# A decode attention kernel with its maximum one chunk later, one wait a head on VectorE, and K0 in one load

## The chip, the cores and the metric

The kernel runs on one core of a Trainium2 chip. The metric is the device time of one execution in microseconds. The kernel before takes 318.31 us, the median of three runs (318.19 to 318.35). The core has a matrix engine (TensorE, PE in the profile), a vector engine (VectorE, DVE), a scalar engine (ScalarE, ACT), GpSimd (POOL), and a queue engine (SyncE, SP) that here issues all loads of K and V. Each works through its own instructions in order; they meet through semaphores.

## What is computed

One query row per head attends to 8192 keys, for 16 heads of width 256, in bfloat16:

```python
B, H, Sq, Sk, D = 1, 16, 1, 8192, 256
def reference(q, k, v):
    scale = q.shape[-1] ** -0.5
    scores = jnp.einsum("bhqd,bhkd->bhqk", q, k) * scale
    p = _softmax(scores, axis=-1)
    return jnp.einsum("bhqk,bhkd->bhqd", p, v)
```

K and V of one head are 4 MB each and are used once, so 134 MB are read.

## The kernel before

A head's keys lie on 128 partitions, 64 keys on each. K and V have two buffers each, by the parity of the head. The SyncE queue issues the loads in the order of the list `ORDER` (L16); it waits, ahead of K(h), until VectorE (semaphore `kd`) and GpSimd (`tp`) have finished head h−2, and ahead of V(h) until TensorE's sum of iteration h is done (`pr`). A wait there holds all loads behind it. `CUTS` (L15) splits some loads into pieces: K0 and K15 after 34 of 64 keys, V13, V14 and V15 in other places. The second piece of a K has the semaphore `kb`.

**The scores.** Of the 64 keys of a partition, the first 24 go to GpSimd and ScalarE: GpSimd multiplies four keys at a time by the head's q row into one of two `prod` buffers (L186, six groups a head), and ScalarE sums each key's products into the score tile S (L398, four instructions a group, then semaphore `sp`). The other 40 go to VectorE: four chunks (index c) of ten fused multiply-and-sum instructions (L212), each chunk followed by semaphore `kd`.

**The maximum.** When VectorE has ended its four chunks, it waits for its own last chunk and for ScalarE's last group and takes the maximum of each partition (L229, semaphore `m`). TensorE turns it into a row (L332, `mT`); VectorE reduces that to one number g (L203, function `xmax`) behind the first chunk of the next head; TensorE spreads it over the partitions (L317, `bc`); ScalarE takes the exponent (L363, function `expo`) in the next head's loop of groups, behind group i = 1.

**The output.** TensorE's iteration h spreads the maximum of head h−1 (L317), multiplies the exponents of head h−2 with V (L270, 32 matmuls), sums the exponents of head h−1 (L257, "the sum"), runs a filler (L281), then waits for ScalarE's `collect` (L374), which copies the product out of PSUM, and gathers its rows (L294). Only then does it wait for the maximum of head h, turn it (L331, L332), and make the broadcast q row of head h+2 (L247). ScalarE's iteration h begins with `q_copy`, the copy of the q row of head h+1 (L392 and L354), which TensorE makes at the end of its iteration h−1; then come the six groups, with `expo` and `final` (L380, the scaled output of an earlier head) between them, and `collect` at the end. The last head's V comes in four pieces, and its last 36 keys are added directly to the output rows (L339).

**The waits at a head's start.** The function `k_waits` (L142 to L144) waits for the q row (`qb`) and for the two K semaphores. VectorE runs it in every chunk (L208), with a further wait for `kb` (L209), and GpSimd in every pair of groups (L183). For head 15, the wait on `kb` passes in the first chunk (c = 0) with K0's second piece alone, and asks for K15's second piece from c = 1 on.

Of the kernel before, what the change touches and what calls it, by code (L numbers as in the profile page):

```python
# [5 lines left out]
ALU = mybir.AluOpType  # L6
ACT = mybir.ActivationFunctionType
AX = mybir.AxisListType
# [13 lines left out]
AHEAD = {"k1": 16, "kb": 16, "sp": 2, "pr": 1, "cm": 2, "pv": 1, "fin": 3, "rc": 3, "ex": 1, "mT": 1, "g": 1, "nb": 1}  # L22
STREAM_AHEAD = ("v0", "v1", "v0_40", "v1_48")


def bass_standalone__mha_softmax__decode_kernel(nc: bass.Bass, q: bass.AP, k: bass.AP, v: bass.AP, out: bass.AP):
# [28 lines left out]
    with contextlib.ExitStack() as ctx:  # L55

        def sb(name, shape, d):
            return ctx.enter_context(nc.sbuf_tensor(name, shape, d))
# [31 lines left out]
        lsum = sb("lsum", [P, 1], FP32)  # L90
        recip = sb("recip", [WIDE, H], FP32)
# [3 lines left out]
        ones_col = sb("ones_col", [P, 1], FP32)  # L95
        o_all = sb("o_all", [WIDE, LAST * HW], out.dtype)
        o_last = sb("o_last", [1, D], out.dtype)

# [5 lines left out]
        qrow = ps("qrow", [P, 2 * 512])  # L104
        spare = ps("spare", [P, 512])

        for name in ("pool", "cb", "cf", "ldq", "qp", "qb", "tp", "sp", "kd", "m", "mT", "g", "bc", "nb", "ex"):
            sem(name)
        for name in ("rc", "pr", "cm", "pv", "fin", "o"):
            sem(name)  # L110
# [30 lines left out]
        def k_waits(e, h):  # L141
            e.wait_ge(sem("qb"), h + 1)  # L142
            e.wait_ge(sem("k0"), h // 2 * 16 + 16)  # L143
            e.wait_ge(sem("k1"), (h + 1) // 2 * 16 + 16)  # L144

        @(lambda f: f(nc.gpsimd))
        def _(pool):
            def step(ins, n):
                ins.then_inc(sem("pool"), 1)
                pool.wait_ge(sem("pool"), n)  # L150

            def eye(t, n, done):
# [18 lines left out]
            pool.memset(ones_col[:, :], 1.0).then_inc(sem("cf"), 1)  # L171
            pool.memset(lsum[:, :], 0.0).then_inc(sem("cf"), 1)
            pool.memset(g[:, :], 0.0).then_inc(sem("cf"), 1)
            pool.memset(comb[:, :], 0.0).then_inc(sem("cf"), 1)
            step(pool.memset(sel[:, :], 0.0), 3)
            for n in range(4):
                step(pool.memset(sel[n * BLK : n * BLK + 1, n % 2 * WIDE : n % 2 * WIDE + 1], 1.0), n + 4)
            pool.memset(E[:, :], 0.0).then_inc(sem("cf"), 1)

            with pool.Fori(0, H) as h:  # L180
                par = pool.snap(h % 2)
                with pool.Fori(0, NG // 2) as i:
                    k_waits(pool, h)  # L183
                    for b in range(2):
                        pool.wait_ge(sem("sp"), h * NG + i * 2 + (b + 1))
                        pool.tensor_tensor(  # L186
                            out=prod[:, b * GRP * D : (b + 1) * GRP * D].rearrange("p (b d) -> p b d", b=GRP),
                            in0=kbuf[:, ds(par * (J * D) + i * (2 * GRP * D) + b * (GRP * D), GRP * D)].rearrange(
                                "p (b d) -> p b d", b=GRP
                            ),  # L190
                            in1=q_now[:, ds(par * D, D)].rearrange("p (b d) -> p b d", b=1).to_broadcast([P, GRP, D]),
                            op=ALU.mult,
                        ).then_inc(sem("tp"), 1)

        @(lambda f: f(nc.vector))
        def _(dve):
            def recips(h, n, after=0):
                dve.wait_ge(sem("pr"), h - n + (3 + after))
                dve.reciprocal(recip[:, ds(back(h, n), 1)], tot[0:WIDE, :]).then_inc(sem("rc"), 1)  # L199

            def xmax(h, n):
                dve.wait_ge(sem("mT"), h - n + 2)
                dve.tensor_reduce(g[:, :], mx[0:1, 0:P], AX.X, ALU.max).then_inc(sem("g"), 1)  # L203

            with dve.Fori(0, H) as h:
                par = dve.snap(h % 2)
                with dve.Fori(0, NC) as c:  # L207
                    k_waits(dve, h)  # L208
                    dve.wait_ge(sem("kb"), (h * 8 + c + 119) // 120 * 16 + 16)  # L209
                    for b in range(CH):  # L210
                        col = kbuf[:, ds(par * (J * D) + c * (CH * D) + (NPL + b) * D, D)]
                        ins = dve.scalar_tensor_tensor(  # L212
                            out=col,
                            in0=col,
                            scalar=SCALE,
                            in1=qrow[:, ds(par * 512, D)],
                            op0=ALU.mult,
                            op1=ALU.mult,
                            accum_out=S[:, ds(h * J + c * CH + (NPL + b), 1)],
                        )  # L220
# [8 lines left out]
                dve.tensor_reduce(m[:, :], S[:, ds(h * J, J)], AX.X, ALU.max).then_inc(sem("m"), 1)  # L229
# [6 lines left out]
            dve.tensor_scalar(  # L236
                out=o_last[:, a : a + HW],
                in0=ob[row : row + 1, 0:HW],
                scalar1=recip[0:1, LAST:H],
                scalar2=None,  # L240
                op0=ALU.mult,
            ).then_inc(sem("fin"), 1)

        @(lambda f: f(nc.tensor))
        def _(pe):
# [59 lines left out]
            pe.wait_ge(sem("cb"), 1)  # L305
            for n in range(2):
                qcast(n, slice(n, n + 1))
            pe.wait_ge(sem("cf"), 7)
# [41 lines left out]
        def _(act):  # L350
# [25 lines left out]
            def final(h, n):  # L376
                act.wait_ge(sem("pv"), h - n + 4)
                act.wait_ge(sem("rc"), h - n + 4)
                i = back(h, n)
                act.activation(  # L380
                    out=o_all[:, ds(i * HW, HW)],
                    in_=ob[0:WIDE, 0:HW],
                    func=ACT.Copy,
                    scale=recip[:, ds(i, 1)],
                ).then_inc(sem("fin"), 1)

            act.dma_start(q_sb[:, :], q[0, :, 0, :]).then_inc(sem("ldq"), 16)
# [2 lines left out]
            with act.Fori(0, H + 2) as h:  # L390
                with act.If(h < H):
                    q_copy(h + 1)  # L392
                with act.Fori(0, NG) as i:
                    with act.If(h < H):
# [21 lines left out]
            act.activation(out=o_last[:, 0:HW], in_=ob[0:1, 0:HW], func=ACT.Copy, scale=recip[0:1, LAST:H]).then_inc(  # L416
                sem("fin"), 1
            )
            act.nop()
# [28 lines left out]
```

## Time and profile before

| | |
|---|---|
| median of 3 runs | 318.31 us |
| profiled execution | 318.05 us |
| its span | 316.6 us |
| VectorE busy | 232.5 us (73%) |
| GpSimd busy | 204.3 us (65%) |
| ScalarE busy | 191.2 us (60%) |
| TensorE busy | 147.2 us (46%) |
| bytes of K and V | 134.23 MB, 424 GB/s over the span |
| largest shares of the chain that ended last | DMA 52%, VectorE 20% |

The span runs from the first to the last recorded instruction of the profiled execution; all times inside it count from its start. In the timeline rows the columns are start, duration, engine, source line, operation, the tile written and the tile read, the number of instructions, and in brackets the idle time ahead of the first with what ended it. A busy share is an average over the whole span, so it doesn't say which engine is waited for at the end. The chain is the path of work back from the last instruction, and a long DMA piece in it covers all that went on at the time.

### The profile page before, as it was taken

To read this page: it belongs to the slowest core of one execution; us is meant where nothing else is said; L and a number is where in the kernel's file an instruction comes from. 1 tells how busy PE (TensorE), PEld (TensorE's weight loads), DVE (VectorE), ACT (ScalarE), POOL (GpSimd) and SP (SyncE) were. 2 spreads that over 40 slices of the span, in tenths; PEclk is the share of its full clock that TensorE was granted. 3 is DMA by queue.
4 is the path that set the end of the run, shared out by engine and by line. 5 is a ranking of instruction groups with operands and counts; after the bars stand their busy time and mean duration, and the time that the engine had idled before them with its cause. 6 is when DMAs were issued, how large, how long until landed. Compare 5 with 4: busy or idle time off the path is not lost.

```text
span 316.6 us, 7885 instructions
## 1 busy us (share of the span) xinstructions
PE 147.2 (46%) x866; PEld 67.0 (21%) x866; DVE 232.5 (73%) x1329; ACT 191.2 (60%) x866; POOL 204.3 (65%) x115
## 2 busy tenths in 40 slices
PE   3201418264262633729191541915428063281977
PEld 1000103022120311314040210402213031130434
DVE  0797979497694967969797969769396793969700
ACT  2476737477373864767767657647386473858521
POOL 3888658395683857869686848568284783886400
PEclk9999999759585585766768585765958558576799
DMA  7999999999999999999999999999999999999996
GB/s 304 430 460 402 460 418 443 426 435 443 418 443 418 455 406 460 402 464 397 464 397 464 397 464 397 464 402 460 402 460 406 455 426 435 408 437 419 433 424 268
DMA packets 5683, 134.25 MB, mean 424 GB/s; under 512 B 673, under 2 KB 690, under 8 KB 946
## 3 DMA queue, kind: packets, MB, share of 16 engines
q1 hardware_dynamic: 5650, 134.23, 98.9%
q8 instruction: 1, 0.02, 0.0%
q10 hardware_dynamic: 32, 0.01, 0.0%
HBM read 134.23 MB, written 0.01 MB: 424 GB/s over the span
## 4 chain that ended last, share of the span: by engine, by line
DMA 52%; DVE 20%; issue 11%; DVEq 9%; PE 2%; POOL 2%; ACT 1%; SPq 1%; ACTq 1%; POOLq 1%
DMA kbuf<-in_k_dram 38%; DVE kbuf L212 19%; DMA vbuf<-in_v_dram 14%; DVEq L212 6%; PE acc L270 2%; POOL prod L186 2%; DVEq L209 1%; ACT prod L398 1%; DVEq L207 1%; DVEq L144 1%; SPq L127 1%; DVEq L143 0%; PE ob L339 0%; ACTq L398 0%; DVE g L203 0%
## 5 line engine op out<-in xcount | busy, mean ns | idle before, releaser
L212 DVE SCALAR_TENSOR_TENSOR kbuf<-kbuf,qrow x640 | 223.7, 416 | 53.7 <-issue 27.7
L186 POOL TENSOR_TENSOR prod<-kbuf,q_now 128x1024 f32 x96 | 201.8, 2123 | 89.7 <-DMA kbuf<-in_k_dram 60.7
L398 ACT ACTIVATE prod<-prod x384 | 154.5, 403 | 74.0 <-POOL prod L186 68.0
L270 PE MATMUL acc<-vbuf,E 128*64 128x512 bf16 x494 | 87.2, 529 | 30.3 <-DMA vbuf<-in_v_dram 29.7
L398 ACT ACTIVATION_READ_ACCUMULATOR prod<-prod x384 | 71.6, 186 | 0.0
L270 PEld LDWEIGHTS acc<-vbuf,E 128*64 128x64 bf16 x494 | 37.1, 150 | 74.1 <-issue 36.0
L212 DVE DVE_READ_ACCUMULATOR kbuf<-kbuf,qrow x640 | 52.6, 82 | 0.0
L317 PE MATMUL mx<-g,ones_row 1*128 1x1 f32 x34 | 9.7, 351 | 75.7 <-DVE g L203 75.4
L294 PE MATMUL ob<-comb,sel 97*1 97x128 f32 (+1 forms) x144 | 20.9, 321 | 35.0 <-ACT comb L374 34.8
L317 PEld LDWEIGHTS mx<-g,ones_row 1*128 1x128 f32 x34 | 8.2, 298 | 79.9 <-DVE g L203 79.2
L354 ACT ACTIVATE q_now<-qrow (+1 forms) x17 | 6.5, 383 | 28.8 <-PE qrow L247 28.7
L281 PE MATMUL spare<-ident 128*128 128x512 f32 x36 | 22.2, 700 | 0.0
L294 PEld LDWEIGHTS ob<-comb,sel 97*1 97x1 f32 (+1 forms) x144 | 8.0, 95 | 57.0 <-ACT comb L374 48.0
L332 PE MATMUL mx<-ident,m 128*1 128x128 f32 x32 | 7.8, 333 | 20.9 <-DVE m L229 20.9
L229 DVE TENSOR_REDUCE m<-S 128x1 f32 x16 | 3.5, 220 | 13.8 <-ACT prod L398 12.6
L374 ACT ACTIVATE comb<-acc 97x512 f32<-97x512 f32 x16 | 9.3, 578 | 6.2 <-PE tot L257 6.2
L363 ACT ACTIVATE E<-S,negb x16 | 9.3, 582 | 4.1 <-ACT negb L360 4.1
L199 DVE RECIPROCAL recip<-tot 33x1 f32 (+1 forms) x16 | 2.5, 155 | 9.8 <-PE tot L257 9.8
L247 PE MATMUL qrow<-q_sb,identb 16*128 16x256 bf16 x18 | 5.9, 337 | 4.6 <-DMA q_sb<-in_q_dram 4.6
L332 PEld LDWEIGHTS mx<-ident,m 128*1 128x1 f32 x32 | 2.9, 95 | 21.9 <-DVE m L229 21.9
L380 ACT ACTIVATE o_all<-ob,recip 33x128 f32 x15 | 5.4, 362 | 1.5 <-PE ob L294 1.5
L281 PEld LDWEIGHTS spare<-ident 128*128 128x128 f32 x36 | 5.8, 201 | 0.3
(27 smaller groups left out, 31.1 us busy)
## 6 DMA issues: line engine op xcount, KB each, us to landing
kbuf<-in_k_dram SPq DMA_DIRECT2D x14, 4096.0 KB, 21.1
vbuf<-in_v_dram SPq DMA_DIRECT2D x13, 4096.0 KB, 27.1
kbuf<-in_k_dram SPq DMA_DIRECT2D x2, 2176.0 KB, 13.3
kbuf<-in_k_dram SPq DMA_DIRECT2D x2, 1920.0 KB, 17.4
vbuf<-in_v_dram SPq DMA_DIRECT2D x1, 3072.0 KB, 29.9
vbuf<-in_v_dram SPq DMA_DIRECT2D x1, 2560.0 KB, 19.4
vbuf<-in_v_dram SPq DMA_DIRECT2D x1, 1792.0 KB, 10.3
vbuf<-in_v_dram SPq DMA_DIRECT2D x1, 1536.0 KB, 22.7
```

Source lines behind the costliest of these rows:

```text
L186: pool.tensor_tensor(out=prod[:, b * GRP * D : (b + 1) * GRP * D].rearrange("p (b d) -> p b d", b=GRP), in0=kbuf[:, ds(par * (J * D) + i * ...
L212: ins = dve.scalar_tensor_tensor(out=col, in0=col, scalar=SCALE, in1=qrow[:, ds(par * 512, D)], op0=ALU.mult, op1=ALU.mult, accum_out=S[:, ...
L247: pe.matmul(qrow[:, ds(at * 512, D)], lhsT=identb[0:H, col].to_broadcast([H, P]), rhs=q_sb[:, :], start=True, stop=True,).then_inc(sem("qp ...
L270: ins = pe.matmul(acc[at : at + STRIP, :], lhsT=E[:, par * EW + j // 2 :][:, 0:STRIP], rhs=vbuf[par][:, j * D : (j + 2) * D], start=(j < 4 ...
L281: pe.matmul(spare[:, :].rearrange("p (b x) -> p b x", x=P), lhsT=ident[:, :], rhs=ident[:, :].rearrange("p (b x) -> p b x", b=1).to_broadc ...
L294: ins = pe.matmul(ob[row : row + wide, 0:HW], lhsT=sel[:, n * WIDE : n * WIDE + wide], rhs=comb[:, n * D + a : n * D + a + HW], start=(n = ...
L317: pe.matmul(sm, lhsT=ones_row[:, :], rhs=g[:, :], start=True, stop=True).then_inc(sem("bc"), 1)
L332: pe.matmul(mx[0:1, 0:P], lhsT=m[:, :], rhs=ident[:, :], start=True, stop=True).then_inc(sem("mT"), 1)
L354: act.activation(out=q_now[:, ds(par * D, D)], in_=qrow[:, ds(par * 512, D)], func=ACT.Copy).then_inc(sem("qb"), 1)
L363: act.activation(out=E[:, ds(i % 2 * EW, J)].rearrange("p (two x) -> p x two", two=2), in_=S[:, ds(i * J, J)].rearrange("p (x two) -> p x ...
L374: act.activation(out=comb[:, :], in_=acc[0:ROWS, :], func=ACT.Copy).then_inc(sem("cm"), 1)
L398: ins = act.activation(out=part, in_=part, func=ACT.Copy, scale=SCALE, accum_out=S[:, ds(back(h, 0) * J + i * GRP + b, 1)],)
```

## The change

- The maximum of head h−1 is taken behind the first chunk of head h (a new helper `maximum`), and the reciprocal and `xmax` move from behind the first to behind the second chunk. For the last head, all of it follows the loop.
- ScalarE's `expo` and `final` move from group i = 1 to group i = 3.
- VectorE's waits in each chunk are replaced by two at a head's start: one for a new semaphore `go`, which GpSimd raises when it has passed its own `k_waits`, and one for `kb`, which for head 15 asks for the whole of K15. GpSimd runs `k_waits` once a head.
- K0 is loaded in one piece.
- `comb` and `sel`, and `lsum` and `ones_col`, share a tile each, so that two fill instructions at the start go; `recip` has one more column, with its index moved by one, and the starting values of two counters follow.

```diff
-CUTS = {"k0": (0, 34), "k15": (0, 34), "v13": (0, 48), "v14": (0, 40), "v15": (0, 28, 48, 60)}
+CUTS = {"k15": (0, 34), "v13": (0, 48), "v14": (0, 40), "v15": (0, 28, 48, 60)}
...
-        comb = sb("comb", [ROWS, 2 * D], FP32)
-        sel = sb("sel", [ROWS, 2 * WIDE], FP32)
+        comb_sel = sb("comb_sel", [ROWS, 2 * D + 2 * WIDE], FP32)
+        comb, sel = comb_sel[:, 0 : 2 * D], comb_sel[:, 2 * D :]
...
             with pool.Fori(0, H) as h:
                 par = pool.snap(h % 2)
+                k_waits(pool, h)
+                pool.nop().then_inc(sem("go"), 1)
                 with pool.Fori(0, NG // 2) as i:
-                    k_waits(pool, h)
...
-                dve.reciprocal(recip[:, ds(back(h, n), 1)], tot[0:WIDE, :]).then_inc(sem("rc"), 1)
+                dve.reciprocal(recip[:, ds(back(h, n - 1), 1)], tot[0:WIDE, :]).then_inc(sem("rc"), 1)
...
+            def maximum(h, n):
+                dve.wait_ge(sem("sp"), h * NG - n * NG + (NG + 2))
+                dve.wait_ge(sem("kd"), h * NC - n * NC + NC)
+                dve.tensor_reduce(m[:, :], S[:, ds(back(h, n) * J, J)], AX.X, ALU.max).then_inc(sem("m"), 1)
+
             with dve.Fori(0, H) as h:
                 par = dve.snap(h % 2)
+                dve.wait_ge(sem("go"), h + 1)
+                dve.wait_ge(sem("kb"), (h + 1) // H * 16 + 16)
+                dve.nop().then_inc(sem("dg"), 1)
                 with dve.Fori(0, NC) as c:
-                    k_waits(dve, h)
-                    dve.wait_ge(sem("kb"), (h * 8 + c + 119) // 120 * 16 + 16)
...
-                    with dve.If(c == 0):
-                        with dve.If(h > 1):
+                    with dve.If(h > 0):
+                        with dve.If(c == 0):
+                            maximum(h, 1)
+                        with dve.If(c == 1):
                             recips(h, 2)
-                        with dve.If(h > 0):
                             xmax(h, 1)
-                dve.wait_ge(sem("kd"), h * NC + NC)
-                dve.wait_ge(sem("sp"), h * NG + (NG + 2))
-                dve.tensor_reduce(m[:, :], S[:, ds(h * J, J)], AX.X, ALU.max).then_inc(sem("m"), 1)
+            maximum(LAST, 0)
             recips(LAST, 1)
             xmax(LAST, 0)
...
-                    with act.If(i == 1):
+                    with act.If(i == 3):
                         with act.If(h > 0):
                             with act.If(h < H + 1):
                                 expo(h, 1)
```

Three places show what moves. The first is VectorE at the start of a head, up to its first product. Before, these rows stood inside the loop of chunks and ran four times a head:

```order
L207 ISA
L143 ISA [waits qb]
L144 ISA [waits k0]
L209 ISA [waits k1]
L212 ISA [waits kb]
L212 ISA x2
L212 SCALAR_TENSOR_TENSOR kbuf,S<-kbuf,qrow 128x256
```

Now the waits for `go` and `kb` stand ahead of the loop of chunks, which begins at L214:

```order
L209 ISA
L212 ISA [waits go]
L214 UNCONDITIONAL_BRANCH [waits kb]
L214 ISA
L217 ISA x2
L217 SCALAR_TENSOR_TENSOR kbuf,S<-kbuf,qrow 128x256
```

Three waits of each chunk have gone, and one for GpSimd's signal has come; the wait for `kb` stays, once a head.

The second is VectorE behind the ten products of a chunk. Before, the reciprocal and the maximum's last step followed the first chunk, and the maximum stood behind the loop (from L227 on):

```order
L199 ISA [waits pr]
L199 RECIPROCAL recip<-tot 33x1
L223 UNCONDITIONAL_BRANCH
L225 COMPARE_AND_BRANCH
L203 TENSOR_REDUCE g<-mx 1x1 [waits mT]
L225 UNCONDITIONAL_BRANCH
L207 REGISTER_ALU
L207 COMPARE_AND_BRANCH
L227 ISA
L228 ISA [waits kd]
L229 ISA [waits sp]
L229 TENSOR_REDUCE m<-S 128x1
```

Now the maximum of the previous head stands in the loop, behind the first chunk, and the two others behind the second:

```order
L205 ISA
L206 REGISTER_ALU [waits sp]
L207 ISA [waits kd]
L207 TENSOR_REDUCE m<-S 128x1
L228 UNCONDITIONAL_BRANCH
L230 COMPARE_AND_BRANCH
L198 ISA [waits pr]
L198 RECIPROCAL recip<-tot 33x1
L202 TENSOR_REDUCE g<-mx 1x1 [waits mT]
L230 UNCONDITIONAL_BRANCH
L214 REGISTER_ALU
L214 COMPARE_AND_BRANCH
```

The maximum moved from the end of its head to a place one chunk into the next.

The third is GpSimd from the start of a head to its first group. Before, the three waits stood inside the loop of pairs of groups (L182):

```order
L182 ISA
L143 ISA [waits qb]
L144 ISA [waits k0]
L185 ISA [waits k1]
L186 ISA [waits sp]
L186 ISA x2
L186 TENSOR_TENSOR prod<-kbuf,q_now 128x1024
```

Now they stand ahead of that loop, with the signal `go` behind them:

```order
L178 ISA
L143 ISA [waits qb]
L144 ISA [waits k0]
L182 UNCONDITIONAL_BRANCH [waits k1]
L182 ISA
L185 ISA [waits sp]
L185 ISA x2
L185 TENSOR_TENSOR prod<-kbuf,q_now 128x1024
```

The waits run once a head instead of three times, and VectorE's signal goes out ahead of the first group.

More of the change, by code (lines that the diff above doesn't have):

```diff
@@ L21 @@
 WIDE = BLK + 1
-AHEAD = {"k1": 16, "kb": 16, "sp": 2, "pr": 1, "cm": 2, "pv": 1, "fin": 3, "rc": 3, "ex": 1, "mT": 1, "g": 1, "nb": 1}
+AHEAD = {"k1": 16, "kb": 16, "sp": 2, "pr": 1, "cm": 2, "pv": 1, "fin": 3, "rc": 2, "ex": 1, "mT": 1, "g": 1, "nb": 1}
 STREAM_AHEAD = ("v0", "v1", "v0_40", "v1_48")
@@ L89, in bass_standalone__mha_softmax__decode_kernel @@
         negb = sb("negb", [P, 1], FP32)
-        lsum = sb("lsum", [P, 1], FP32)
-        recip = sb("recip", [WIDE, H], FP32)
+        lsum_ones = sb("lsum_ones", [P, 2], FP32)
+        lsum, ones_col = lsum_ones[:, 0:1], lsum_ones[:, 1:2]
+        recip = sb("recip", [WIDE, H + 1], FP32)
         ident = sb("ident", [P, P], FP32)
@@ L94, in bass_standalone__mha_softmax__decode_kernel @@
         ones_row = sb("ones_row", [1, P], FP32)
-        ones_col = sb("ones_col", [P, 1], FP32)
         o_all = sb("o_all", [WIDE, LAST * HW], out.dtype)
@@ L105, in bass_standalone__mha_softmax__decode_kernel @@
         spare = ps("spare", [P, 512])
-        for name in ("pool", "cb", "cf", "ldq", "qp", "qb", "tp", "sp", "kd", "m", "mT", "g", "bc", "nb", "ex"):
+        for name in ("pool", "cb", "cf", "ldq", "qp", "qb", "go", "dg", "tp", "sp", "kd", "m", "mT", "g", "bc", "nb", "ex"):
             sem(name)
@@ L170, in _ @@
             pool.memset(ones_row[:, :], 1.0).then_inc(sem("cf"), 1)
-            pool.memset(ones_col[:, :], 1.0).then_inc(sem("cf"), 1)
-            pool.memset(lsum[:, :], 0.0).then_inc(sem("cf"), 1)
+            pool.memset(lsum_ones[:, :], 1.0).then_inc(sem("cf"), 1)
             pool.memset(g[:, :], 0.0).then_inc(sem("cf"), 1)
-            pool.memset(comb[:, :], 0.0).then_inc(sem("cf"), 1)
-            step(pool.memset(sel[:, :], 0.0), 3)
+            step(pool.memset(comb_sel[:, :], 0.0), 3)
             for n in range(4):
@@ L238, in _ @@
                 in0=ob[row : row + 1, 0:HW],
-                scalar1=recip[0:1, LAST:H],
+                scalar1=recip[0:1, H : H + 1],
                 scalar2=None,
@@ L307, in _ @@
                 qcast(n, slice(n, n + 1))
-            pe.wait_ge(sem("cf"), 7)
+            pe.wait_ge(sem("cf"), 5)
             cut13, cut14, cuts = CUTS["v13"][1], CUTS["v14"][1], CUTS["v15"]
@@ L383, in final @@
                     func=ACT.Copy,
-                    scale=recip[:, ds(i, 1)],
+                    scale=recip[:, ds(i + 1, 1)],
                 ).then_inc(sem("fin"), 1)
@@ L415, in _ @@
             act.wait_ge(sem("rc"), H + 3)
-            act.activation(out=o_last[:, 0:HW], in_=ob[0:1, 0:HW], func=ACT.Copy, scale=recip[0:1, LAST:H]).then_inc(
+            act.activation(out=o_last[:, 0:HW], in_=ob[0:1, 0:HW], func=ACT.Copy, scale=recip[0:1, H : H + 1]).then_inc(
                 sem("fin"), 1
```

## Prediction

> **What bounds the kernel now.** First the page's span, its DMA row and the bytes.
>
> ```profile
> span 316.6 us, 7885 instructions
> DMA  7999999999999999999999999999999999999996
> HBM read 134.23 MB, written 0.01 MB: 424 GB/s over the span
> ```
>
> Of 40 slices only the first and the last show DMA engines below nine tenths. The stream of K and V is dense from beginning to end; no compute engine sets the middle. A compute change can then matter in three ways: a transfer is issued so late that the queue runs dry, the work before the first byte changes, or the work behind the last bytes does. So the next view is the end of the chain that ended last (start, duration, what), and TensorE's own timeline there.
>
> ```profile
> 262.44 29.90 DMA vbuf<-in_v_dram
> 292.39 6.20 PE acc L270 x32
> 298.65 0.33 SPq L127
> ...
> 299.50 14.39 DMA vbuf<-in_v_dram
> 313.93 1.08 PE ob L339 x32
> ```
>
> ```profile
> 298.55 1.13 PE L281 MATMUL spare<-ident 128*128 128x512 f32 x2
> 299.60 0.82 PE L294 MATMUL ob<-comb,sel 97*33 97x128 f32 x7
> ...
> 300.48 0.28 PE L247 MATMUL qrow<-q_sb,identb 16*128 16x256 bf16 x1
> ...
> 301.45 2.35 PE L270 MATMUL acc<-vbuf,E 128*64 128x512 bf16 x20
> 304.66 1.49 PE L270 MATMUL acc<-vbuf,E 128*64 128x512 bf16 x12 [0.86 <-DMA vbuf<-in_v_dram]
> ...
> 308.95 1.70 PE L270 MATMUL acc<-vbuf,E 128*64 128x512 bf16 x14 [0.85 <-DMA vbuf<-in_v_dram]
> ...
> 313.93 1.06 PE L339 MATMUL ob<-vbuf,E 128*1 128x128 bf16 x32 [0.20 <-DMA vbuf<-in_v_dram]
> ```
>
> From 298 us on TensorE runs one serial program (gather of head 13, the product of head 14, its gather, head 15) and waits for data only three times: 0.86 + 0.85 + 0.20 = 1.91 us. That is the whole cover of the tail. If ScalarE's collect of head 13, which starts the gather, comes later by d, the kernel ends later by d − 1.91.
>
> **The change, part by part.**
>
> *The maximum behind the next head's first chunk.* This reaches further than VectorE. TensorE makes the q row of head h+2 (L247) behind its wait for the maximum of head h (L331). ScalarE begins iteration h+1 with the copy of that row (L392), and all its products of head h+1 stand behind the copy in its queue. So ScalarE now starts a head only after VectorE's first chunk of the same head; behind it wait six groups of products, the exponent, final and collect, and GpSimd too, which has two prod buffers and stops after two groups. Before, the maximum fell at the end of the previous head. In the last head:
>
> ```profile
> 284.15 0.38 ACT L354 ACTIVATE q_now<-qrow  x1 [1.46 <-PE qrow L247]
> 284.72 0.42 ACT L398 ACTIVATE prod<-prod  x1 [0.18 <-issue]
> ...
> 288.55 0.17 ACT L360 ACTIVATE negb<-mx 128x1 f32<-128x1 f32 x1 [0.53 <-PE mx L317]
> 288.98 0.58 ACT L363 ACTIVATE E<-S,negb  x1 [0.26 <-ACT negb L360]
> ...
> 290.06 0.42 ACT L398 ACTIVATE prod<-prod  x1 [0.36 <-issue]
> ...
> 297.93 0.40 ACT L398 ACTIVATE prod<-prod  x1
> 298.65 0.60 ACT L374 ACTIVATE comb<-acc 97x512 f32<-97x512 f32 x1 [0.23 <-PE tot L257]
> ```
>
> ```profile
> 284.11 0.42 DVE L212 SCALAR_TENSOR_TENSOR kbuf<-kbuf,qrow  x1 [1.53 <-issue]
> ...
> 287.53 0.15 DVE L199 RECIPROCAL recip<-tot 33x1 f32 x1
> ```
>
> ScalarE's products ran from 284.72 to 298.33, collect began at 298.65. The new times:
>
> K15's landing comes first, since VectorE now waits for both pieces of K15 (semaphore kb) ahead of the first chunk. The first 3072 KB piece of V13 follows K15 in the stream and landed at 262.44 + 29.90 = 292.34; 3.15 MB at 424 GB/s are 7.4 us, so K15 was complete at 284.9.
>
> ```profile
> vbuf<-in_v_dram SPq DMA_DIRECT2D x1, 3072.0 KB, 29.9
> ```
>
> From a landing to VectorE's first product: K0's second piece landed at 1.20 + 11.78 = 12.98, the product started at 13.60, 0.6 us.
>
> ```profile
> 0.74 0.40 SPq L127
> ...
> 1.20 11.78 DMA kbuf<-in_k_dram
> ...
> 13.60 0.17 DVE kbuf L212
> ```
>
> So VectorE starts at 285.6 instead of 284.11. One chunk is 287.53 − 284.11 = 3.4 us, and I take 0.3 for the branch and the two waits, bounded by nothing and by 1.53 (the idle time at the head's start, which held five waits): the maximum at 289.3. From a maximum to ScalarE's copy, where TensorE was free, head 0 shows 26.04 − 24.60 = 1.44 us:
>
> ```profile
> 24.60 0.22 DVE L229 TENSOR_REDUCE m<-S 128x1 f32 x1 [0.30 <-ACT prod L398]
> ```
>
> ```profile
> 26.04 0.38 ACT L354 ACTIVATE q_now<-qrow  x1 [1.59 <-PE qrow L247]
> ```
>
> The copy at 290.75, the first product 0.57 later (284.72 − 284.15) at 291.3. Then the six groups.
>
> ```profile
> 286.89 4.20 POOL L186 TENSOR_TENSOR prod<-kbuf,q_now 128x1024 f32 x2 [1.63 <-ACT prod L398]
> 292.24 4.21 POOL L186 TENSOR_TENSOR prod<-kbuf,q_now 128x1024 f32 x2 [1.15 <-ACT prod L398]
> ```
>
> They took 298.33 − 284.72 = 13.6 us, GpSimd's 2.1 us per group alternating with ScalarE's 1.6. With the exponent behind the fourth group instead of the second, the third starts 0.7 earlier (when GpSimd's third ends, 289.0, plus 0.4 of handover, instead of 290.06), and the exponent gives 0.3 back: 13.2 us, bounds 12.9 and 13.9. ScalarE ends at 304.5, and collect starts 0.3 later, at 304.8: 304.8 − 298.65 = 6.15 late. Less the cover of 1.91: **+4.2 us**, bounds 3.5 and 5.5.
>
> V15's issue (298.65) follows the sum of iteration 15, which now waits for the exponent behind the fourth group. That group ends 8.4 us after the first began (GpSimd's fourth ends at 286.89 + 4.20, 6.4 after 284.72, then 0.4 of handover and 1.6 of products); the exponent is done 1.0 later (0.17 + 0.26 + 0.58), the sum and the issue some 0.25 later: 291.3 + 9.65 = 300.95. V14 is in transfer until 304.66, so this costs nothing.
>
> *TensorE's clock in that gap.* TensorE's filler ended 1.0 us after V15's issue (298.55 + 1.13 against 298.65), so now at 302.0; the gather starts 0.95 after collect (299.60 − 298.65), at 305.75. That is a hole of 3.75 us, and behind it 1.85 us of small matmuls (299.60 to 301.45). Two pairs of stretches of the kernel before, cut where its clock changes (length, then busy time and count of PE, PEld, DVE, ACT and POOL, then the granted clock):
>
> ```profile
> 242.99:246.40 3.41, 1.15 (x11) 0.50 (x11) 0.22 (x1) 1.23 (x4) 0.00 (x0) 1.00 0.92 394
> 246.40:249.81 3.41, 0.00 (x0) 0.00 (x0) 2.81 (x17) 0.70 (x3) 3.08 (x2) 0.50 1.07 461
> ...
> 294.19:297.60 3.41, 3.41 (x20) 1.43 (x18) 3.31 (x21) 2.59 (x13) 2.25 (x2) 0.50 0.98 420
> 297.60:301.01 3.41, 3.21 (x26) 1.38 (x22) 1.69 (x11) 1.42 (x6) 0.00 (x0) 1.00 0.95 404
> ```
>
> After 3.41 us with 1.15 busy the clock fell to half; after 3.41 fully busy it returned. In the new gap almost any such stretch holds at most 1.2 busy, so I expect it to fall. The price: 32 matmuls from 292.39 took 6.20, of which 0.99 at full clock at 2.35/20 = 0.12 each; the other 24 took 5.2, 0.22 each. Head 14's product, 32 matmuls, would run 1 to 4 us at half clock: 0.5 to 1.8 lost. Its gather too:
>
> ```profile
> 59.14 1.37 PE L294 MATMUL ob<-comb,sel 97*33 97x128 f32 x7 [4.79 <-ACT comb L374]
> ```
>
> 1.37 instead of 0.82, 0.55 more. Together **+1.7**, bounds 0 and 2.4. The Trainium skill, "TensorE: Matmul & The Clock Gate", Part 1, says the clock falls back after at least one idle window of about 3.4 us. Read strictly, a hole of 3.75 us seldom contains a whole window, which is the rival *warm* below; the first pair of rows speaks against the strict reading, since a third of that window was busy.
>
> *K0 in one piece, and the later V issues.* VectorE's head 0 starts at 13.6 and ends after four chunks of (24.33 − 13.60)/3 = 3.58: 27.9 instead of 24.33. Head 1 starts at 28.4. In each head ScalarE's first group starts 5.7 us after VectorE (291.3 − 285.6), and GpSimd's last group ends 11.0 after that (292.24 + 4.21 − 284.72, less the 0.7), so head 1 ends at 45.1 and head 2 starts at 45.7. V2 waits for the sum of iteration 2, behind the exponent of head 1: 45.7 + 5.7 + 9.65 = 61.05, instead of 53.33.
>
> ```profile
> 24.33 17.79 DMA kbuf<-in_k_dram
> ```
>
> ```profile
> 53.33 0.33 SPq L127 DMA_DIRECT2D vbuf<-in_v_dram  x1
> ```
>
> ```profile
> 62.16 2.12 POOL L186 TENSOR_TENSOR prod<-kbuf,q_now 128x1024 f32 x1 [5.53 <-DMA kbuf<-in_k_dram]
> ```
>
> K3, ahead of it in the queue, lands 0.4 to 0.7 ahead of GpSimd's start at 62.16. A first byte follows an issue by about 0.5 (0.74 to 1.20 at the start). So V2's bytes start at 61.55 where the queue ends at about 61.5. Later, K7 and K8 have two transfers (19.6 us) between their release and the end of the queue; the release now comes 18.1 after a landing (1.2 to VectorE's start, an estimate: the 0.6 above and as much for GpSimd's waits and signal; 16.7 to GpSimd's end; 0.2 to the issue), 1.0 in hand after the 0.5. Elsewhere a third transfer lies between. I take **+0.5** for the stream, bounds 0 and 3.
>
> *VectorE's waits.* Four sets of waits a chunk become one a head, and the wait at a head's end (1.2 us) goes. Nothing gained: VectorE is waiting for K while the DMA row is full. The new wait for GpSimd's signal holds the whole head behind it; GpSimd reaches a head before VectorE ends the previous one except where it now ends later, which is counted above. The merged memsets, recip's extra column and the reduced counts lie before K0 lands, or change no instruction on the path: nothing, as long as the 11.8 us to K0's landing cover them.
>
> *Sum.* 4.2 + 1.7 + 0.5 = 6.4. The profiled execution took 318.05 (span 316.6 and 1.45 around it), 0.26 below the median of 318.31. 318.05 + 6.4 = 324.45; against the median **324.7**.
>
> **Rivals.**
>
> *Warm* (18%): the clock does not fall. 318.31 + 4.7 = 323.0. For it: the hole is hardly longer than one such stretch. Against it: the row with 1.15 busy.
>
> *Dry* (18%): the release of K7, K8 and V2 comes 2 to 3 us later than chained, the queue stands still, everything behind moves: +2.5, 327.2. For it: margins below 1 us. Against it: they are spent in few places, and a stall at one gives the next more room.
>
> *Covered* (8%): not slower, 318.3. The tail's transfers hide ScalarE's lateness, as the full DMA row suggests for any engine. This holds if collect of head 13 starts by 298.65 + 1.91 = 300.56, that is, if ScalarE's last head starts by 287.1. Its copy would have to leave before VectorE's first chunk ends, so the wait for the maximum would have to be met earlier than I read it. With the gain of VectorE's waits it could end some tenths faster, but not below the last byte at 313.9.
>
> **How the numbers follow.** Clock falling, forecast: 52%, 324.7, itself 323.3 to 326. Another 4% lies between covered and warm. The range 321.5 to 328.0 takes in warm, the forecast, and dry up to 0.8 us above its price. A measurement of this kernel tells about 0.2% (0.6 us) from no change: faster 2%, same 7%, slower 91%.
>
> **What would show it.** ScalarE's first product of each head should start some 5.7 us behind VectorE's first, with GpSimd idle after two groups. The last collect-to-gather hole on TensorE should be near 3.6 us, with the clock at one half when head 14's product begins; V15's landing should stay near 314 with TensorE ending some 5 us behind it. A DMA row with a slice below nine tenths in the middle is *dry*. If the waits on V14 and V15 are still there, the chain through ScalarE's copy is wrong.

## The result, and the profile after

The changed kernel takes 328.96 us, the median of 5 runs (326.71 to 330.79); the kernel before 318.31 us (318.19 to 318.67). The ratio is 1.033, with a 95% interval of 1.028 to 1.038: slower, as forecast, but by 10.65 us where 6.4 were forecast, and outside the range. The runs also spread by 4 us where those of before spread by half a microsecond. The profiled execution (330.79 us) is the longest of the five, so its terms are the upper end.

The same lines of the page as before, for the changed kernel:

```profile
span 328.9 us, 7665 instructions
DMA  8999999999999999999999999999999999999970
HBM read 134.23 MB, written 0.01 MB: 408 GB/s over the span
```

The DMA row still shows no slice below nine tenths in the middle, and yet the mean rate fell from 424 to 408 GB/s. Part of that is the tail, in which nothing is loaded: the last load lands 8.4 us ahead of the span's end, 2.1 us before. The rest is in the middle, where the row counts a packet that is waiting as busy (a packet is one of the pieces, here mostly of 32 KB, in which a DMA engine moves a load). The rate shows what the row hides. Stretches of 2 us of the changed kernel (the last two columns are the DMA share and GB/s):

```profile
118.00:120.00 2.00, 1.03 (x2) 0.20 (x2) 0.00 (x0) 1.74 (x9) 1.38 (x1) 1.00 0.92 393
120.00:122.00 2.00, 0.00 (x0) 0.00 (x0) 0.00 (x0) 2.00 (x9) 0.00 (x0) 1.00 0.92 262
...
140.00:142.00 2.00, 0.00 (x0) 0.00 (x0) 2.00 (x13) 2.00 (x12) 1.08 (x1) 1.00 0.87 246
```

At 120 and 140 us the share is near 0.9 while the rate is some 60% of the usual. These are the first bytes of K7 and K8. The SyncE queue's timeline has the issues:

```profile
58.40 0.33 SPq L127 DMA_DIRECT2D vbuf<-in_v_dram  x1
...
98.70 0.33 SPq L127 DMA_DIRECT2D vbuf<-in_v_dram  x1
100.15 19.63 SPq L127 DMA_DIRECT2D kbuf<-in_k_dram  x2
...
139.96 0.33 SPq L127 DMA_DIRECT2D kbuf<-in_k_dram  x1
```

V2 was issued at 58.40, K7 at 100.15 + 19.63 − 0.33 = 119.45, K8 at 139.96. The trace also has every single packet, and for each load the moment at which each of the 16 DMA engines reports that its share has landed. Worked out from these records:

```
                                        before     after
issue of V2 / K7 / K8, us               53.33 / 115.87 / 135.44     58.40 / 119.45 / 139.96
transfer ahead lands, first to last
of the 16 DMA engines                   61.2-61.5 / 119.5-119.8 / 138.9-139.3   61.1-61.5 / 120.3-122.4 / 140.9-142.7
packets over 0.2 us too long,
between 3.5 and 300 us                  0          56
a 32 KB packet as a rule / a slow one   1.22 us    1.21 us / 1.4 to 2.8 us
mean of the 16 landings later than
before, for V2 / V4 / K7 / K8 / K13     -          0.79 / 1.14 / 2.09 / 3.47 / 3.47 us
K15's second piece lands, first to last 284.7-285.0    287.9-291.0
```

Two losses in one: the landings are 3.5 us late on the mean, and the 16 engines, which land within 0.4 us of each other before, have come 3.1 us out of step by K8 and stay so as far as V14. A wait for a transfer waits for the last engine, so K15 is ready 291.0 − 285.0 = 6.0 us late. A fourth late issue lost a little too: V4's, at 98.70, 1.75 us ahead of the first landing of K5.

Then the tail. ScalarE, VectorE and TensorE in the last head (timelines):

```profile
296.69 0.38 ACT L358 ACTIVATE q_now<-qrow  x1 [5.00 <-PE qrow L251]
297.25 0.42 ACT L402 ACTIVATE prod<-prod  x1 [0.18 <-issue]
...
309.86 0.40 ACT L402 ACTIVATE prod<-prod  x1
310.26 0.57 ACT L378 ACTIVATE comb_sel<-acc 97x512 f32<-97x512 f32 x1
```

```profile
291.83 0.42 DVE L217 SCALAR_TENSOR_TENSOR kbuf<-kbuf,qrow  x1 [5.02 <-DMA kbuf<-in_k_dram]
...
295.25 0.21 DVE L207 TENSOR_REDUCE m<-S 128x1 f32 x1
```

```profile
306.69 1.12 PE L285 MATMUL spare<-ident 128*128 128x512 f32 x2
310.89 1.36 PE L298 MATMUL ob<-comb_sel 97*33 97x128 f32 x7 [3.07 <-ACT comb_sel L378]
...
313.38 5.66 PE L274 MATMUL acc<-vbuf,E 128*64 128x512 bf16 x32
...
325.11 2.27 PE L343 MATMUL ob<-vbuf,E 128*1 128x128 bf16 x71
```

ScalarE waits 5.00 us for the q row, starts 5.4 us behind VectorE, and TensorE waits 3.07 us for collect, now without any wait for data behind it. The clock in TensorE's hole and behind it, cut where it changes (the share of full speed is the column ahead of the last two):

```profile
307.26:310.68 3.42, 0.56 (x2) 0.00 (x0) 0.29 (x2) 3.42 (x17) 0.92 (x1) 1.00 0.89 309
310.68:314.09 3.41, 3.12 (x17) 1.50 (x19) 0.28 (x1) 0.49 (x3) 0.00 (x0) 0.50 1.02 432
314.09:317.50 3.41, 3.41 (x18) 1.43 (x16) 0.00 (x0) 0.62 (x3) 0.00 (x0) 0.50 0.96 404
```

It fell at 310.68 and stayed at half until 317.50. Head 13's gather and head 14's product took from 310.89 to 319.04, 8.15 us; before, they took from 299.60 to 306.15, 5.69 us without the wait for data of 0.86 us in them.

### The profile page after: what moved, and what is told of

Same layout as the page of the kernel before. It is cut to its first block, busy times and chain, and to the rows that moved or that the text cites. A ratio compares the mean times of both kernels' runs of the same rounds, so it can differ in the third digit from the quotient of the medians.

```text
span 328.9 us, 7665 instructions
## 1 busy us (share of the span) xinstructions
PE 160.3 (49%) x866; PEld 68.5 (21%) x866; DVE 226.9 (69%) x1330; ACT 190.1 (58%) x866; POOL 204.2 (62%) x113
## 4 chain that ended last, share of the span: by engine, by line
DMA 42%; POOL 17%; issue 11%; DVE 7%; PE 6%; ACT 6%; DVEq 4%; ACTq 4%; POOLq 2%; SPq 0%
DMA kbuf<-in_k_dram 42%; POOL prod L185 17%; DVE kbuf L217 7%; ACT prod L402 5%; DVEq L217 2%; PE acc L274 2%; PE mx L336 1%; ACTq L402 1%; DVEq L214 1%; POOLq L185 1%; PE ob L298 1%; PE qrow L251 1%; POOLq L182 1%; PE ob L343 1%; ACTq L399 1%
## 5 line engine op out<-in xcount | busy, mean ns | idle before, releaser
L274 PE MATMUL acc<-vbuf,E 128*64 128x512 bf16 x494 | 90.0, 544 | 6.2 <-DMA vbuf<-in_v_dram 4.9
L217 DVE DVE_READ_ACCUMULATOR kbuf<-kbuf,qrow x640 | 49.3, 77 | 0.0
L298 PE MATMUL ob<-comb_sel 97*1 97x128 f32 (+1 forms) x144 | 21.6, 331 | 41.7 <-ACT comb_sel L378 41.5
L336 PE MATMUL mx<-ident,m 128*1 128x128 f32 x32 | 9.0, 381 | 56.6 <-DVE m L207 56.6
L298 PEld LDWEIGHTS ob<-comb_sel 97*1 97x1 f32 (+1 forms) x144 | 8.1, 96 | 64.4 <-ACT comb_sel L378 54.8
L336 PEld LDWEIGHTS mx<-ident,m 128*1 128x1 f32 x32 | 1.6, 84 | 62.1 <-DVE m L207 62.1
L378 ACT ACTIVATE comb_sel<-acc 97x512 f32<-97x512 f32 x16 | 9.2, 575 | 5.5 <-PE tot L261 5.5
L261 PE MATMUL tot<-lsum_ones 128*33 128x1 f32 x36 | 4.0, 180 | 14.0 <-ACT E L367 14.0
L261 PEld LDWEIGHTS tot<-lsum_ones 128*33 128x33 f32 x36 | 3.0, 113 | 20.2 <-ACT E L367 19.1
## 6 DMA issues: line engine op xcount, KB each, us to landing
vbuf<-in_v_dram SPq DMA_DIRECT2D x1, 2560.0 KB, 19.2
```

The lines of the kernel that those rows point to most:

```text
L217: ins = dve.scalar_tensor_tensor(out=col, in0=col, scalar=SCALE, in1=qrow[:, ds(par * 512, D)], op0=ALU.mult, op1=ALU.mult, accum_out=S[:, ...
L261: pe.matmul(tot[0:WIDE, :], lhsT=lsum[:, :].to_broadcast([P, WIDE]), rhs=ones_col[:, :], start=True, stop=True,).then_inc(sem("pr"), 1)
L274: ins = pe.matmul(acc[at : at + STRIP, :], lhsT=E[:, par * EW + j // 2 :][:, 0:STRIP], rhs=vbuf[par][:, j * D : (j + 2) * D], start=(j < 4 ...
L298: ins = pe.matmul(ob[row : row + wide, 0:HW], lhsT=sel[:, n * WIDE : n * WIDE + wide], rhs=comb[:, n * D + a : n * D + a + HW], start=(n = ...
L336: pe.matmul(mx[0:1, 0:P], lhsT=m[:, :], rhs=ident[:, :], start=True, stop=True).then_inc(sem("mT"), 1)
L378: act.activation(out=comb[:, :], in_=acc[0:ROWS, :], func=ACT.Copy).then_inc(sem("cm"), 1)
```

## The experiments

Theory A: ScalarE's copy of the next q row, which now stands behind the maximum, causes both losses, the late issues and the late last head. Theory B: the other parts of the change do. Theory L, for the step that had failed: an issue needs far more than 0.5 us of lead.

**1. The q row ahead of the maximum's wait, in the changed kernel.**

```diff
-                    pe.wait_ge(sem("m"), h + 1)
-                    pe.matmul(mx[0:1, 0:P], lhsT=m[:, :], rhs=ident[:, :], start=True, stop=True).then_inc(sem("mT"), 1)
+                    pe.wait_ge(sem("kd"), h * NC + NC)
                     qcast(par, ds(h + 2, 1))
+                    pe.wait_ge(sem("m"), h + 1)
+                    pe.matmul(mx[0:1, 0:P], lhsT=m[:, :], rhs=ident[:, :], start=True, stop=True).then_inc(sem("mT"), 1)
```

The added wait for `kd` keeps the row that VectorE is still reading from being overwritten.

> The changed kernel, but TensorE makes the q row of head h+2 behind VectorE's last chunk of head h, ahead of its wait for the maximum. Theory A (ScalarE's copy standing behind the maximum causes both the late releases and the late last head): ScalarE starts each head within 2 us of the K landing again, the packets keep their 1.2 us throughout, and the time returns to 318 to 320 us. Theory B (the other parts of the change, K0 in one piece, the exponent two groups later, VectorE's waits for GpSimd and for all of K15, carry the loss): it stays at 325 us or more.

Measured 318.52 us (10 runs, 318.36 to 319.39), ratio to before 1.0003 (0.9994 to 1.0013), no slow packet. In its last head the copy leaves early, VectorE starting later than ScalarE's copy:

```profile
283.99 0.38 ACT L359 ACTIVATE q_now<-qrow  x1 [1.45 <-PE qrow L251]
```

```profile
286.00 0.42 DVE L217 SCALAR_TENSOR_TENSOR kbuf<-kbuf,qrow  x1 [5.03 <-DMA kbuf<-in_k_dram]
```

The maximum stays behind the next head's first chunk, and the whole loss is gone. Theory A holds for all of it: none of the other parts costs anything that can be measured while the copy is early.

**2. The maximum back at the end of its head, all else changed.**

```diff
                     with dve.If(h > 0):
                         with dve.If(c == 0):
-                            maximum(h, 1)
-                        with dve.If(c == 1):
                             recips(h, 2)
                             xmax(h, 1)
-            maximum(LAST, 0)
+                maximum(h, 0)
```

> The changed kernel with the maximum back at the end of its own head, and the reciprocal and the last step back behind the first chunk; all other parts of the change stay. Theory A: 318 to 320 us, as with the q row made first. Theory B: 325 us or more. If the place of the maximum itself costs something beyond the copy, this one is faster than the one with the q row first by more than 1 us.

318.73 us (10 runs), ratio 1.0011 (1.0002 to 1.0021): as the first, within 0.2 us. The place of the maximum costs nothing beyond the copy.

**3. The maximum's move alone, in the kernel before**, with the change's helper `maximum`.

```diff
...
                     with dve.If(c == 0):
+                        with dve.If(h > 0):
+                            maximum(h, 1)
+                    with dve.If(c == 1):
                         with dve.If(h > 1):
                             recips(h, 2)
                         with dve.If(h > 0):
                             xmax(h, 1)
-                dve.wait_ge(sem("kd"), h * NC + NC)
-                dve.wait_ge(sem("sp"), h * NG + (NG + 2))
-                dve.tensor_reduce(m[:, :], S[:, ds(h * J, J)], AX.X, ALU.max).then_inc(sem("m"), 1)
+            maximum(LAST, 0)
```

> The kernel before with nothing changed but the place of the maximum (behind the next head's first chunk) and of the two steps behind it (second chunk); K0 in two pieces, the exponent behind the second group, and all waits as before. Theory A: most of the loss, 323 to 327 us: the last head's ScalarE ends some 5 us later, and packets of 2 us appear around K7 and K8, though not at V2. Theory B: 318 to 320 us.

322.41 us (4 runs, 320.2 to 323.05), ratio 1.011 (1.007 to 1.016). Most slow packets stand at 119 and 139 us, a few at 80 and 100 us, none at V2; K15 lands at 288.2. Neither theory's number: A's range began at 323. The move alone carries some 4 of the 10.65 us. The rest needs the move and another part together, since experiments 1 and 2 show that the other parts without the late copy cost nothing.

**4 and 5. Which other part multiplies it.** In the changed kernel, first the exponent back behind the second group, then K0 in two pieces and the wait for second pieces in the chunks.

```diff
-                    with act.If(i == 3):
+                    with act.If(i == 1):
```

> The changed kernel with the exponent and the final output back behind the second group. Theory A: V2 and V4 are issued some 1 us earlier, the stall at 61 us shrinks or goes, K7, K8 and the last head stay late: 325 to 328 us. Rival (the late V issues are the loss): 319 to 322 us.

```diff
+CUTS = {"k0": (0, 34), "k15": (0, 34), "v13": (0, 48), "v14": (0, 40), "v15": (0, 28, 48, 60)}
...
-                dve.wait_ge(sem("kb"), (h + 1) // H * 16 + 16)
...
                 with dve.Fori(0, NC) as c:
+                    dve.wait_ge(sem("kb"), (h * 8 + c + 119) // 120 * 16 + 16)
```

> The changed kernel with K0 in two pieces again and VectorE's wait for the second piece in each chunk, so that head 0 and head 15 start on their first piece. Theory A: head 2 starts about 1 us earlier and V2 is issued with 4 us to spare, and the last head's copy leaves 1.5 us earlier; K7 and K8 stay late: 324.5 to 327 us. Rival (K0 and K15 in whole are the loss): 318 to 320 us.

The exponent: 327.87 us (4 runs, ratio 1.031, 1.029 to 1.033), a gain that the runs do not separate from none. In the profile, which is of the fastest of the four, V2 was issued at 57.75, lost 0.2 us on the mean there instead of 0.9, and K15 landed at 287.5. The pieces: 323.67 us (321.65 to 325.84, ratio 1.018, 1.012 to 1.024), a gain of 5, more than A expected.

**6. K15's second piece alone.**

```diff
-                dve.wait_ge(sem("kb"), (h + 1) // H * 16 + 16)
...
                 with dve.Fori(0, NC) as c:
+                    dve.wait_ge(sem("kb"), (h * NC + c + 3) // 64 * 16 + 16)
```

> The changed kernel, with VectorE's wait for the second piece of K15 back in the chunks, so that head 15 starts on its first piece; K0 stays in one piece. Theory A: ScalarE's last copy leaves some 3 us earlier, collect of head 13 starts 15 to 16 us behind K15's landing instead of 19.3, the holes on TensorE shrink; the late K7 and K8 stay: 324 to 326 us. If what restoring both K0's and K15's pieces gained came from K0: 328 us or more.

324.14 us (322.55 to 326.83, ratio 1.018, 1.012 to 1.025). That is the gain of experiment 5 as near as the runs can tell, so it comes from K15, not K0: the late stream is still there (some 60 slow packets, K15 landing at 291.6), and the gain is in the tail. VectorE of this kernel, then its collect of head 13, in the last head:

```profile
289.04 0.42 DVE L217 SCALAR_TENSOR_TENSOR kbuf<-kbuf,qrow  x1 [1.46 <-DMA kbuf<-in_k_dram]
292.46 0.21 DVE L207 TENSOR_REDUCE m<-S 128x1 f32 x1
...
307.34 0.57 ACT L378 ACTIVATE comb_sel<-acc 97x512 f32<-97x512 f32 x1
```

The maximum comes 0.9 us behind K15's full landing where it came 4.2 behind in the changed kernel (295.25 − 291.02), and collect starts at 307.34, 15.8 us behind that landing instead of 19.2. With the copy behind the first chunk, a wait ahead of that chunk is passed on to ScalarE in full.

**7 to 10. What a late issue costs, in the kernel before.** Only one issue is made to wait for a later event; V2 twice, K7 twice.

```diff
                         sp.wait_ge(sem("pr"), h + 2)
+                        if h == 2:
+                            sp.wait_ge(sem("sp"), 3 * NG + 2)
```

> The kernel before, but the issue of V2 waits for ScalarE's last group of head 2, so that it comes at about 58.6 us instead of 53.3, 2.9 us ahead of the landing of K3 (61.5), as in the changed kernel. Theory L (an issue less than some 3 us ahead of the end of the queue starves the DMA engines although the queue is never empty by the issue times, and leaves them out of step): 2 us packets at 60 to 62 us, the last landing of each later transfer 1.5 us or more behind its first, and 320 to 322 us. The step of my prediction (a first byte follows an issue by 0.5 us): no slow packet, 318.3 us.

```diff
                         sp.wait_ge(sem("pr"), h + 2)
+                        if h == 2:
+                            sp.wait_ge(sem("tp"), 3 * NG)
```

> The kernel before, but the issue of V2 waits for GpSimd's last group of head 2, so that it comes at about 56.7 us, 4.8 us ahead of the landing of K3. Theory L: this lead is enough, no packet above 1.3 us in the middle, 318.3 us within 0.5. If any later issue of V2 costs something, 319 us or more.

```diff
                         sp.wait_ge(sem("tp"), (h - 1) * NG)
+                        if h == 7:
+                            sp.wait_ge(sem("mT"), 7)
```

> The kernel before, but the issue of K7 waits for TensorE's turned maximum of head 5, so that it comes at about 118.9 us instead of 115.9, 0.6 to 0.9 us ahead of the landing of K6 (119.5 to 119.8), as K7 and K8 in the changed kernel. Nothing else is later. Theory L (late issue alone makes the loss): packets of 2 us at 119 to 121 us, the stream behind shifted by 1 us or more, engines out of step by 1 us or more to the end, 319.5 to 321.5 us. If an issue that still comes ahead of the landing costs nothing, 318.3 us.

```diff
                         sp.wait_ge(sem("tp"), (h - 1) * NG)
+                        if h == 7:
+                            sp.wait_ge(sem("sp"), 6 * NG + 2)
```

> The kernel before, but the issue of K7 waits for ScalarE's last group of head 5, so that it comes at about 117.0 us, 2.5 us ahead of the landing of K6. Theory L with the bound as V2's late issue in the kernel before showed it (2.5 us of lead were enough in most runs): 318.3 to 319.0 us, no or few slow packets. If a lead of 2.5 us starves the engines: 319.5 us or more.

```
late issue        at, us   ahead of the predecessor's landing   time, us (runs)           ratio, 95%
V2                58.73    2.5 (first engine) to 2.9 (last)     318.48 (318.19-319.12)    1.0004, 0.9994-1.0013
V2                56.78    4.4 to 4.8                           318.27 (318.21-318.32)    0.9996, 0.9986-1.0006
K7                118.88   0.6 to 1.1                           320.09 (319.75-320.31)    1.0056, 1.0039-1.0073
K7                117.05   2.4 to 2.8                           319.88 (319.4-320.35)     1.0049, 1.0032-1.0065
K7 before         115.87   3.6 to 4.0                           318.31                    -
```

The same two stretches, before, then with K7 issued at 118.88, then at 117.05:

```profile
118.00:120.00 2.00, 1.39 (x10) 0.46 (x9) 0.00 (x0) 0.36 (x1) 0.00 (x0) 0.50 0.80 344
120.00:122.00 2.00, 0.00 (x0) 0.00 (x0) 1.12 (x7) 0.02 (x1) 1.42 (x1) 0.50 1.22 524
```

```profile
118.00:120.00 2.00, 1.09 (x10) 0.32 (x9) 0.00 (x0) 0.38 (x1) 0.00 (x0) 0.55 0.79 262
120.00:122.00 2.00, 0.00 (x0) 0.00 (x0) 1.00 (x5) 0.00 (x0) 1.30 (x1) 0.50 0.94 344
```

```profile
118.00:120.00 2.00, 0.92 (x9) 0.23 (x5) 0.00 (x0) 0.38 (x1) 0.00 (x0) 0.54 0.91 377
120.00:122.00 2.00, 0.00 (x0) 0.00 (x0) 1.12 (x7) 0.00 (x0) 1.42 (x1) 0.50 1.10 459
```

One issue of K7, a single time in the program, still ahead of its predecessor's landing, costs 1.4 to 1.6 us of the whole, against the 318.46 of the kernel before in the same set of runs. The two do it differently. At 0.6 us of lead all engines stop: the landings are 1.4 us late on the mean, and stay within 0.5 us of each other. At 2.4 us the mean is only 0.2 to 0.3 us late, but part of the engines fall behind: the landings are 2.0 us apart from K7 on to the end. V2 with 2.5 us of lead cost nothing: no slow packet, and its longest run, 319.12, is no longer than the longest of the kernel before in that set, 319.15. So Theory L, as it was put for V2, is not borne out there; for K7 it is.

All profiles together say how far the lead decides. For the 26 loads from V0 to V12 and K2 to K14, 4 MB each, of the 13 other kernels, take each one's lead over the first landing of the load ahead of it, and the lateness that it adds: how much later than in the kernel before its 16 landings came on the mean, less the same for the load ahead:

```
lead, us        loads    added lateness of that one load, us
under 1.0       10       0.86 to 1.88, every one
1.0 to 2.0      8        0.06 to 0.85
2.0 to 3.4      18       0.00 to 0.89
3.4 and more    302      none above 0.03
```

In the band between 1 and 3.4 us the lead alone does not settle it: V2 with 2.7 us lost 0.89 us in the changed kernel and with 2.8 us 0.02 us in experiment 5. What else decides there stays open.

**11 and 12. TensorE's clock.** The changed kernel with the filler three times, in all iterations and then in iteration 15 alone.

```diff
                 keep_running()
+                keep_running()
+                keep_running()
                 pe.wait_ge(sem("cm"), h + 1)
```

> The changed kernel with the filler three times instead of once in each of TensorE's iterations, which fills the 3 us hole ahead of the last gathers. Clock theory: the clock stays whole through head 14's product, TensorE's end comes 2 to 3 us less behind the last collect (17.1 us in the changed kernel, 14.5 to 15.2 here), time 325.5 to 327.5 us. Rival (the clock in the hole costs nothing, the filler only delays): 329 to 331 us.

```diff
                 keep_running()
+                with pe.If(h == LAST):
+                    keep_running()
+                    keep_running()
                 pe.wait_ge(sem("cm"), h + 1)
```

> The changed kernel with the filler three times in TensorE's iteration 15 alone, ahead of the gather that waits for the last collect. Clock theory: from that gather's start to the end of head 14's product 5.5 us instead of 8.2, time 325.5 to 327 us. Rival: no change, 328 to 330 us.

With the filler everywhere, 328.29 us (4 runs, 327.44 to 329.2). Its TensorE timeline:

```profile
309.03 0.82 PE L298 MATMUL ob<-comb_sel 97*33 97x128 f32 x7 [1.35 <-ACT comb_sel L380]
...
310.88 3.65 PE L274 MATMUL acc<-vbuf,E 128*64 128x512 bf16 x32
```

From the gather's start to the end of the product 5.50 us instead of 8.15: the clock stayed whole, and the half clock's price is 2.65 us. The total lies between the two expectations: two later fillers, 1.7 us longer each, then stand on the path and take the gain back. In iteration 15 alone: 327.73 us (327.18 to 328.07), again between the expectations. That piece took 7.15 us where 5.5 were expected, the clock falling all the same, but later, at 311.0, for 3.4 us:

```profile
309.18 0.82 PE L298 MATMUL ob<-comb_sel 97*33 97x128 f32 x7 [1.34 <-ACT comb_sel L381]
...
311.02 5.31 PE L274 MATMUL acc<-vbuf,E 128*64 128x512 bf16 x32
```

So the price of the half clock on that piece is shown; that the total gets it back is not, since the runs overlap those of the changed kernel.

No version here beats the kernel before by more than the measurement tells; the first experiment equals it.

## Why the prediction was wrong, step by step

The profiled execution's span grew by 328.9 − 316.6 = 12.3 us. By the prediction's terms, from the rows above:

```
term                                            predicted   measured (profiled execution)
K15's landing later (the stream)                +0.5        291.0 - 285.0 = +6.0
collect later, counted from K15's landing       +6.15       (310.26 - 291.02) - (298.65 - 285.0) = +5.6
the tail's cover                                -1.91       -1.9 (no wait for data is left)
TensorE's clock                                 +1.7        8.15 - 5.50 = +2.65
sum                                             +6.4        +12.35
```

The tail by itself (the last three terms) grew by 6.35 us where 5.9 were forecast; nearly all of the miss is the first term. That the sum closes to a tenth is partly luck: terms that the table leaves out cancel (the gather follows collect's start by 0.63 us, not 0.95; head 13's gather and head 14's product took 2.46 us longer than before, not 2.65; what follows that product took some 0.5 us longer).

- **The bound was read rightly**: the stream sets the middle, so a compute change acts through late issues, the opening or the tail.
- **The copy behind the maximum** is the root, and experiment 1 shows it with a single edit. The chain from the landing held step by step: 0.8 us to VectorE's start (0.6 forecast), 3.4 to the maximum (3.7), 1.44 to the copy (1.44), 13.0 from the first product to collect (13.5).
- **The clock** fell as the row with 1.15 busy suggested. The stretch of 3.42 us that let it fall held 0.56 us of work, so no whole idle window was needed. The Trainium skill's rule in "TensorE: Matmul & The Clock Gate", Part 1, taken strictly, would have kept it whole; the trace decides against that reading. The clock's price came out beyond the upper bound of 2.4, because the half clock lasted 6.8 us, through nearly all of the product.
- **The wait for the whole of K15** was counted for its 1.5 us on VectorE. Experiment 6 puts its share in the tail at some 3.4 us of collect (19.2 against 15.8 behind the landing): with the wait back in the chunks VectorE started 2.5 us ahead of the full landing, not 0.8 behind it, where the kernel before started only 0.9 ahead. In the changed kernel it had ended head 14 at 286.81 and stood idle for 5.02 us.
- **The step that failed** is the sentence "A first byte follows an issue by about 0.5 (0.74 to 1.20 at the start)", and with it the term of +0.5 for the stream. The chain's row at 1.20 is not a first byte: 1.20 is where the issue of K0's second piece begins. The first packet of K0 starts at 1.76, 1.0 us behind the first issue, and takes 1.0 to 1.5 us for 17 KB, where the same packet takes 0.65 later. The leads themselves came out near the forecast or better: K7 and K8 were to be issued 1.5 us ahead of the end of the queue and were, counted to the first and the last landing, 0.8 to 2.9 and 0.9 to 2.7 us ahead of it; V2 was to have 0.5 and had 2.7 to 3.1. By the sentence each of these was in time; measured, V2, K7 and K8 lost 0.9, 0.9 and 1.4 us on the mean, and V4, which the prediction did not name, 0.4. That makes 3.6 us, or 3.5 with the 0.1 us by which the stream had been early; the engines' falling out of step makes it 6.0 at K15's last landing.
- **The rival *dry*** named the place and the sign, but not the way: its condition, releases 2 to 3 us later than chained, did not occur (V2 came 2.65 us earlier, K7 17.5 us behind K5's last landing where 18.1 were chained), its price of +2.5 has no term for engines out of step, and the sign that it was to be known by, a slice of the DMA row below nine tenths, did not show.
- **V15's issue** was put at nothing, because V14 was to be in transfer still. It came at 306.80, 0.6 us ahead of V14's first landing, and V15's first piece lost another 1.1 us on the mean. It cost nothing all the same: its last landing, 314.86, came 6.0 us later than before, as V14's did by then, and TensorE did not wait for it.

## What to carry to other kernels

When a step is moved behind a wait, look for everything that its engine's partners issue behind the same wait: here a copy of the next head's input stood behind a maximum that had nothing to do with it, and ordering the two the other way round gives the whole loss back. In a kernel bound by a stream of loads, count the lead of each issue over the landing of the transfer ahead of it; here 3.4 us and more were safe, less than 1 us never was, and between the two it varied. A full DMA busy row does not prove a dense stream: compare the rate too.

## What the runs showed of the hardware

- A DMA engine whose queue is refilled late is shown as busy: packets of 32 KB that take 1.21 us appear with 1.4 to 2.8 us, and 56 of them, together 2.4 us of all 16 engines' time, made most of the 3.5 us that the stream lost in the changed kernel.
- Being issued ahead of the landing before it does not keep a load dense: of 10 loads with less than 1 us of lead each lost 0.9 us or more, of 302 with 3.4 us or more none lost over 0.03.
- Engines once out of step stay so in a dense stream: with K7 issued at 117.05, a spread of 2.0 us at K7 was still 2.0 us at the first piece of V15, 180 us later, with no late issue in between.
- A spread lengthens the waits and not only the end: with the mean 0.2 to 0.3 us late, the same kernel took 1.4 us more.
